# A retention recurrence and a gelu feed-forward on one core: the hand-written order made anew, rows of chunks 3 to 5 over three queues, part 0 of w_in batch by batch in chunk 0

## The chip, the cores and the metric

The kernel runs on one core of one Trainium2 chip. A core has five engines that work side by side: TensorE (PE: matrix products out of SBUF into PSUM banks), VectorE (DVE), ScalarE (ACT), GpSimd (POOL) and SyncE (SP), which here only issues transfers. Each engine executes its own instructions in the order in which the program lists them. Transfers are moved by 16 DMA engines; an engine that issues one puts it in its own queue. The metric is the device time of one execution in microseconds (us), lower is better; the time before is a median of three runs.

## The reference

Two stages follow each other. The first is a recurrence per batch and head with a decay, the second a feed-forward with a tanh gelu on the first one's output. B = 4 batches, H = 8 heads, S = 768 tokens, D = 64.

```python
gamma = 1.0 - 2.0 ** (-5.0 - np.arange(H))
scale = 1.0 / np.sqrt(D)
for t in range(S):
    state = gamma[None, :, None, None] * state + np.einsum('bhd,bhe->bhde', k[:, :, t], v[:, :, t])
    y[:, :, t] = scale * np.einsum('bhd,bhde->bhe', q[:, :, t], state)
x = y.transpose(0, 2, 1, 3).reshape(B * S, H * D)          # 3072 x 512
h = x @ w_in                                               # w_in 512 x 2048
g = 0.5 * h * (1.0 + np.tanh(c * (h + 0.044715 * h * h * h)))   # c = sqrt(2 / pi)
out = g @ w_out                                            # w_out 2048 x 512, out 3072 x 512, f32
```

All inputs are f32. Inside the kernel the products are made in f16 with f32 sums.

## The kernel before

**Tiling.** The 768 tokens are cut into six chunks of 128. In a chunk the recurrence becomes products of 128 tokens with 128 tokens under a triangular mask with the decay in it, and a state of 64 x 64 per head carries what came before. So there are 24 pairs of a chunk c and a batch b. x of a chunk holds all four batches: 512 columns. The feed-forward goes chunk by chunk; w_in and w_out are each cut into four parts j of 512 of the 2048 inner columns.

**The order.** Nothing is scheduled by a compiler. A string, ORDER (lines 16 to 136), lists 1,125 words; the loop at lines 656 to 661 calls a small function for each word, in that order. A word such as `L:k,3,0,A@9` names the function (L), its arguments (row k of chunk 3, batch 0), where there is a choice the engine that does it (A ScalarE, V VectorE, P GpSimd, S SyncE), and behind the `@` the buffers that it takes. So the string sets the order on each engine, the engine of each movable step, the queue of each transfer and which buffer is used again when.

**The steps of the recurrence**, for chunk c and batch b:

- L (306 to 308): a transfer of one 256 KB row of q, k or v, f32, by the queue named. The destination is one of 13 buffers r.
- PREP (318): the row scaled and made f16, or only made f16. q and k give qk.
- T and ET (chunks 0 and 1): qk transposed by TensorE into a bank and copied out. DT (chunks 2 to 5, 343): the same by a DMA transpose, always issued by SyncE.
- A (350): the scores into two banks; EA (358): the banks times mask, on VectorE, one for each of two groups of heads.
- YP (366): what the state gives; YI (382): what the chunk's own tokens give. EY (chunk 0, 400) and EP (chunks 1 to 5, 403) take the result into x.
- SS (411) and ES (424): the new state. For chunks 1 to 5 one ES is four instructions on VectorE.

**The steps of the feed-forward.** LWI and LWO (258, 266) load one part of w_in or w_out, with a change to f16, through GpSimd's queue; HOLD (272) is a tiny transfer by SyncE that reads one part. A product of chunk and part is made in Strassen's manner with seven products of half the size, M1:c,j,1 to 7 (515), in place of eight. They need sums of weights, WI and WO (300, 304), and sums of x, SX:c,1 to 4 (503). Of one chunk and part the seven M1 collect in three banks, X, Y and Z. CP (543) copies a bank to h, D1 (547, VectorE) adds another to it, G (551, ScalarE) makes the gelu: three CP, three D1 and four G for a chunk and part. In chunk 0 a part can also be made without sums, batch by batch: HB:j,b (462) is 16 products into one bank, and GB:j,b,phi (476) two gelus straight from that bank, each half the size of a G. The second product follows for chunk 0 by O0 (570), EO and ST0 (copy and store), for the others by sums SG:c,j,1 to 4 (555) of the gelus, M2 (590, seven products, each in four pieces), CO (a copy, 636), D2 (an addition on VectorE) and ST (the store).

One instruction is counted by TensorE for each column block: an M1 or M2 is four matmuls of 256 columns, an HB 16 of 128, an O0 four of 512. `mm` is line 219, `tt` (additions and scalings) 216, `copy_on` 211 and 213, the gelu 442, the transposes of T 338, so most rows of the profile have one of these lines.

**Around the change.** In the order before, part 0 of w_in in chunk 0 (at M1:0,0,n) is made for all four batches together in seven products, part 1 (HB:1,b) batch by batch, parts 2 and 3 in seven products. The 36 rows of chunks 3 to 5 are all issued by SyncE, and the transposes DT and all HOLD stand in the same queue. The rows of chunks 0 to 2 go over several queues: GpSimd's has, in this order, v,0,3, then part 0, v,0,0, parts 2, 3 and 1 of w_in, six rows of chunk 1, w_out part 0, the row q,1,0 and so on. Two kinds of queue have landing semaphores of their own: eight are shared by the transfers of SyncE and ScalarE in turn, eight serve GpSimd's; a transfer that takes one waits until the transfer that had it before has landed.

Of the kernel before, what the change touches and what calls it, by code (L numbers as in the profile page):

```python
# [40 lines left out]
WI:1,3,V M1:1,3,2@7 O0:0,2 PREP:k,2,3,P@0 D1:1,3,11 O0:0,3 M1:1,1,5@7 G:1,3,11@16 ES:1,0,V EO:0,V@0 M1:1,3,5@2
PREP:k,2,1,A@2 M1:1,3,6 M1:1,0,2@4 CP:1,3,22,A@2 D1:1,1,11 WO:0,1,P G:1,1,11@17 PREP:q,2,3,P SX:1,4,P@1 O0:1,3
DT:2,3@1 CP:1,1,22,V@0 WO:3,1,P D1:1,0,11 PREP:k,2,2,A@3 L:v,2,1,S@6 M1:1,0,6 O0:2,0@6 CP:1,3,12,V@3
PREP:q,2,2,P PREP:v,2,2,P@0 M1:1,0,5@4 PREP:k,2,0,A@4 G:1,0,11@18 M1:1,3,7 M1:1,3,3 PREP:q,2,1,A CP:1,0,12,A@1
WI:1,2,V O0:2,1 PREP:q,2,0,P DT:2,1@2 DT:2,2@3 D1:1,3,22 LD:S D1:1,3,12 M1:1,1,6 EO:1,A@1 DT:2,0@0 HOLD:1,3
M1:1,1,3 L:v,3,3,S@1 WO:3,2,P G:1,3,22@19 CP:1,1,12,A@2 M1:1,0,7 WI:1,4,P G:1,3,12@20 M1:1,3,4 D1:1,1,12
G:1,3,21@21 A:2,3@2,5 M1:1,1,7 M1:1,2,5@7 O0:2,2 M1:1,2,1@1 EA:2,3,1@0 CP:1,0,22,A@3 PREP:v,2,1,P@3 D1:1,0,22
D1:1,1,22 WO:1,2,P G:1,1,12@22 G:1,1,22@23 EA:2,3,0 M1:1,0,3 L:k,3,0,S@2 M1:1,0,4 D1:1,0,12 O0:2,3
CP:1,2,22,V@2 CP:1,2,11,A@0 L:k,3,2,S@8 L:v,3,0,S@3 G:1,0,21@24 M1:1,1,4 M1:1,2,6 L:q,3,3,S@11 A:2,1@5,2
G:1,1,21@25 PREP:v,3,2,P@2 A:2,2@4,3 L:q,4,1,S@7 EO:2,V@2 EA:2,1,0@3 EA:2,2,1@1 G:1,0,22@26 A:2,0@0,6  # L50
CP:1,2,12,A@3 G:1,0,12@27 PREP:v,2,0,P@1 WO:0,2,P EA:2,0,0@2 L:q,3,2,S@5 PREP:v,2,3,P@4 M1:1,2,3 O0:3,0@5
O0:3,1 EA:2,0,1 L:q,3,0,S@4 M1:1,2,7 PREP:k,3,0,A@1 EA:2,1,1 YP:2,0@3,0 EA:2,2,0 L:k,3,3,S@0 L:k,5,1,S@6
# [12 lines left out]
D2:1,11, DT:3,3@6 M1:2,3,3 M1:2,3,4 DT:3,1@0 D1:2,3,12 M1:2,1,1@6 G:2,0,21@14 L:v,4,0,S@10 M1:2,1,2@0
CP:2,1,22,V@3 CO:1,22,A@5 G:2,3,21@4 SG:1,2,4,P@5 CP:2,1,11,A@1 M2:1,6,1,0 M2:1,3,0,0 SG:1,2,3,V@7 M2:1,6,1,1
# [625 lines left out]
```

## Time and profile before

| | before |
|---|---|
| median of the runs, us | 202.04 (201.94 to 203.08, 3 runs) |
| profiled execution, us | 200.09 |
| its span, us | 198.3 |
| mean granted clock of TensorE | 0.98 |
| busy, us (share): TensorE products | 183.0 (92%) |
| VectorE | 160.0 (81%) |
| GpSimd | 139.1 (70%) |
| ScalarE | 119.3 (60%) |

The profile is one execution; its times start at the span's beginning. In the page each engine's busy tenths stand for 40 equal slices of the span, some 5 us each. A row of the timeline gives the start, the time, the engine (PEld is TensorE's loading of weights, an engine name with a q its issuing of transfers), the line, the operation, out<-in with partitions x elements and type, the number of instructions put together, and in brackets the idle time ahead of it with what ended it. In the grouped rows behind the count stand busy us, mean ns of one, and the idle time with its releasers. A row of the chain of waits has the start, the time and what the chain went through. In the stretches, each engine's us and number of instructions are in the order PE, PEld, DVE, ACT, POOL.

### The profile page before, as it was taken

The page shows a single profiled execution, that of the slowest core. Times are in us where ns is not written, and L with a number is a line of the kernel's source. Part 1 is how long each engine was busy: PE and PEld are TensorE (multiplying, and loading weights), DVE is VectorE, ACT ScalarE, POOL GpSimd, SP SyncE. Part 2 cuts the span into 40 slices and gives each one's busy share as a digit, 9 for nine tenths or more (in the row PEclk, how much of TensorE's full clock was granted, in tenths as well). Part 3 has the DMA queues.
Part 4 walks back from the last instruction along what each step waited for, and adds up shares of the span by engine and source line. Part 5 has one row for each costly group of instructions (what it writes and reads, how often), then busy time and mean ns, then how long its engine had stood idle before and what let it go on. Part 6 is the DMA issues. An engine that isn't in the chain of part 4 may idle for free.

```text
span 198.3 us, 5294 instructions
## 1 busy us (share of the span) xinstructions
PE 183.0 (92%) x2111; PEld 149.0 (75%) x2111; DVE 160.0 (81%) x294; ACT 119.3 (60%) x219; POOL 139.1 (70%) x143
## 2 busy tenths in 40 slices
PE   7377999998999999999999699999999999999992
PEld 2155878575676788877978588878888888888882
DVE  0888979899678999998989999998897577674630
ACT  1329798687767477945784669676544745435111
POOL 0797477977999976973799595898359867447200
PEclk9958999999999999999999999999999999999998
DMA  6999999999989999999999995260200201301453
GB/s 144 288 239 243 203 334 234 295 239 333 270 195 235 214 211 258 213 212 216 244 226 190 209 178 155 53 150 27 94 0 0 86 23 58 106 0 56 141 201 136
DMA packets 80540, 34.26 MB, mean 173 GB/s; under 512 B 69060, under 2 KB 78404, under 8 KB 80516
## 3 DMA queue, kind: packets, MB, share of 16 engines
q1 hardware_dynamic: 66164, 19.35, 44.4%
q0 software_dynamic: 6128, 10.23, 21.7%
q10 hardware_dynamic: 8224, 4.36, 7.6%
q8 instruction: 16, 0.26, 0.5%
q14 instruction: 8, 0.07, 0.1%
HBM read 27.63 MB, written 6.29 MB: 171 GB/s over the span
## 4 chain that ended last, share of the span: by engine, by line
PE 65%; DMA 19%; POOL 6%; DVE 4%; issue 2%; ACT 1%; ACTq 0%; SPq 0%; POOLq 0%; DVEq 0%
PE bank L219 65%; DMA w_in<-in_moe_w_in_dram 9%; DMA r<-in_q_dram 6%; DMA qkT<-qk 2%; DVE g L216 2%; DMA r<-in_v_dram 2%; POOL sx L216 2%; POOL t_out L216 1%; POOL qk L216 1%; POOL v L216 1%; DVE h L216 1%; DVE w_out L216 1%; POOL g L216 1%; POOL w_in L262 0%; POOL qk L213 0%
## 5 line engine op out<-in xcount | busy, mean ns | idle before, releaser
L219 PEld LDWEIGHTS <-g 128*128 128x128 f16 x624 | 60.4, 98 | 11.8 <-PE bank L338 0.3
L216 POOL TENSOR_TENSOR g<-g 128x512 f16<-128x512 f16 x46 | 54.5, 1204 | 17.9 <-DVE g L216 7.2
L219 PE MATMUL bank<-w_out,g 128*128 128x256 f16 (+1 forms) x384 | 60.4, 290 | 0.2 <-DMA w_out<-in_moe_w_out_dram 0.2
L216 DVE TENSOR_TENSOR h<-bank,h 128x512 f32<-128x512 f32 x69 | 46.0, 682 | 8.8 <-PE bank L219 4.4
L442 ACT ACTIVATE g<-h 128x512 f16<-128x512 f32 x69 | 42.7, 634 | 15.4 <-DVE h L216 15.0
L219 PEld LDWEIGHTS <-w_in 128*128 128x128 f16 x432 | 39.2, 98 | 6.2 <-issue 0.8
L211 ACT COPY h<-bank 128x512 f32<-128x512 f32 x57 | 32.7, 588 | 13.0 <-PE bank L219 12.6
L219 PEld LDWEIGHTS <-t_in 128*128 128x128 f16 x276 | 26.4, 98 | 9.9 <-issue 4.3
L219 PE MATMUL bank<-t_out,g 128*128 128x256 f16 x240 | 33.4, 273 | 0.0
L216 DVE TENSOR_TENSOR a<-bank,mask 128x512 f16<-128x512 f32 x48 | 30.0, 680 | 3.5 <-PE bank L219 3.4
L219 PE MATMUL bank<-x,w_in 128*128 128x256 f16 (+1 forms) x248 | 29.7, 259 | 0.4 <-DMA w_in<-in_moe_w_in_dram 0.2
L219 PE MATMUL bank<-sx,t_in 128*128 128x256 f16 x184 | 26.5, 273 | 2.3 <-ACT g L442 1.2
L219 PE MATMUL bank<-sx,w_in 128*128 128x256 f16 x184 | 26.7, 273 | 0.0
L216 DVE TENSOR_TENSOR g<-g 128x512 f16<-128x512 f16 x34 | 22.1, 669 | 3.1 <-ACT g L442 2.1
L442 ACT ACTIVATE g<-bank 128x512 f16<-128x512 f32 (+1 forms) x31 | 16.5, 549 | 8.4 <-PE bank L219 5.8
L211 ACT COPY o<-bank 128x512 f32<-128x512 f32 (+1 forms) x19 | 9.7, 516 | 18.2 <-PE bank L219 18.2
L216 POOL TENSOR_TENSOR v<-r,cst 128x512 f16<-128x512 f32 x16 | 16.9, 1061 | 4.0 <-DMA r<-in_v_dram 4.0
L216 DVE TENSOR_TENSOR o<-bank,o 128x512 f32<-128x512 f32 (+1 forms) x18 | 10.6, 595 | 8.9 <-PE bank L219 8.7
L211 ACT CAST qk<-r 128x512 f16<-128x512 f32 x20 | 12.1, 620 | 6.2 <-PE bank L219 2.2
L219 PE MATMUL bank<-x,t_in 128*128 128x256 f16 x92 | 13.8, 273 | 1.9 <-DVE h L216 1.9
L216 DVE TENSOR_TENSOR qk<-r,cst 128x512 f16<-128x512 f32 x13 | 9.2, 744 | 6.5 <-DMA cst<-rr_cst 4.1
L211 ACT COPY qkT<-bank 128x1024 f16<-128x1024 f16 x7 | 6.9, 1013 | 8.0 <-PE bank L338 8.0
(53 smaller groups left out, 191.9 us busy)
## 6 DMA issues: line engine op xcount, KB each, us to landing
r<-in_v_dram SPq DMA_DIRECT2D x15, 256.0 KB, 4.8
r<-in_q_dram SPq DMA_DIRECT2D x15, 256.0 KB, 4.2
r<-in_k_dram SPq DMA_DIRECT2D x14, 256.0 KB, 4.6
out_dram<-o ACTq DMA_DIRECT2D x11, 256.0 KB, 3.8
r<-in_v_dram POOLq DMA_DIRECT2D x9, 256.0 KB, 8.3
out_dram<-o SPq DMA_DIRECT2D x9, 256.0 KB, 2.3
w_in<-in_moe_w_in_dram POOLq DMA_DIRECT2D x8, 256.0 KB, 9.6
r<-in_k_dram POOLq DMA_DIRECT2D x8, 256.0 KB, 8.6
```

What stands on the lines that cost most here:

```text
L211: nc.scalar.copy(out=out, in_=in_)
L216: EN[e].tensor_tensor(out=out, in0=in0, in1=in1, op=op)
L219: nc.tensor.matmul(out=out, lhsT=lhsT, rhs=rhs, start=start, stop=stop, skip_group_check=True)
L442: nc.scalar.activation(out=out, in_=in_, func=AF.Gelu_apprx_tanh, scale=1.0)
```

## The change

Only the string ORDER differs: 121 lines became 120, and every function is as it was (the lines below the string move up by one). The words are in another order almost throughout, and the buffers behind the `@` are others. What was taken out, put in and given to another engine:

- **Part 0 of w_in in chunk 0**: seven M1:0,0,n, three CP:0,0,n, three D1:0,0,n and four G:0,0,n are gone; HB:0,0 to HB:0,3 and the eight GB:0,b,phi come. Parts 0 and 1 are now both made batch by batch. Sums SX of chunk 0 now serve parts 2 and 3 alone.
- **Rows of chunks 3 to 5**: of 36 on SyncE 21 stay; 11 go to ScalarE's queue (k,3,2 q,3,1 k,3,0 k,3,1 q,3,3 v,3,3 v,3,0 v,3,1 k,4,3 q,5,1 k,5,2), 4 to GpSimd's (k,5,1 k,4,2 v,4,2 q,5,3).
- **Late rows of chunk 0**: k,0,3, q,0,3 and v,0,3 go through GpSimd's queue, among the parts of w_in. There the order is now k,0,3 q,0,3, part 0, v,0,3, parts 2, 3 and 1, then five rows of chunk 1 (k,1,0 k,1,1 q,1,1 q,1,2 q,1,0), w_out part 0, k,1,3 k,1,2 q,1,3, w_out parts 1 and 2, the v rows of chunk 1, with a row of chunk 2 and w_out part 3 behind v,1,3. The row q,1,3 was on SyncE before, and w_out's part 2 stood behind the v rows.
- **Other engines for the same steps**, in number of instructions: SX on VectorE 12 to 17, on GpSimd 12 to 7 (SX:1,2 among them); CP on ScalarE 57 to 49, on VectorE 12 to 17; CO on VectorE 7 to 9; ET on ScalarE 7 to 5, on VectorE 1 to 3; WO on VectorE 5 to 7, on GpSimd 11 to 9; PREP on GpSimd 34 to 37, on VectorE 13 to 11, on ScalarE 25 to 24; one SG from GpSimd to VectorE; one EP, EO and EY and one ES of chunk 0 change engines.
- **The end**: the last steps are made by another order of M2 of chunks 4 and 5; the last copy is CO:5,21,A,0 on ScalarE, with ST:5,21,A,0 behind it, where before D2:5,12,1 on VectorE and ST:5,12,S,1 were last.

In all D1 goes from 69 to 66, G from 92 to 88, M1 from 161 to 154, HB from 4 to 8 and GB from 8 to 16; M2 (140) and O0 (16) stay.

The diff at the start and around chunk 1's loads:

```diff
 ORDER = """
-L:k,0,2,A@0 L:q,0,2,A@1 ZERO L:k,0,0,S@2 SPIN:11@0 LI:A L:q,0,3,A@3 LC:S TABLE PREP:k,0,0,V@0 L:k,0,3,A@4
-L:q,0,1,A@5 L:v,0,1,S@6 PREP:q,0,2,P@1 LWI:0 PREP:k,0,2,V L:v,0,3,P@7 MASK L:k,0,1,S@8 L:q,0,0,S@9
...
-EY:0,0,A EY:0,1,A L:k,1,0,P@3 SS:0,0 WI:0,3,V M1:0,0,5@2 M1:0,0,1@7 WI:0,4,V SX:0,2,V@1 SX:0,3,V@2
-CP:0,0,11,A@0 L:k,1,3,P@4 SX:0,4,V@3 L:k,1,2,P@9 M1:0,0,2@5 M1:0,2,1@1 LWO:0 M1:0,0,6 WI:2,1,V CP:0,0,22,A@1
-CP:0,2,11,A@2 D1:0,0,11 M1:0,2,2@4 WI:2,3,V M1:0,2,5@0 M1:0,0,3 CP:0,0,12,A@3 L:q,1,0,P@8 LWO:1 WI:2,2,V
-L:v,1,2,P@5 D1:0,2,11 G:0,0,11@0 CP:0,2,22,A@0 D1:0,0,12 M1:0,0,7 M1:0,2,6 G:0,2,11@1 ES:0,1,A L:v,1,3,P@11
-G:0,0,12@2 D1:0,0,22 L:v,1,1,P@10 L:v,1,0,P@6 M1:0,2,3 M1:0,3,2@5 WI:3,1,V CP:0,2,12,A@2 M1:0,0,4 M1:0,3,1@4
...
+L:k,0,0,S@0 LC:S L:k,0,2,S@1 ZERO L:q,0,0,S@2 PREP:k,0,0,P@0 L:q,0,2,A@3 TABLE L:k,0,3,P@4 PREP:q,0,2,V@1
+L:q,0,1,A@5 PREP:q,0,1,V@2 PREP:k,0,2,V LI:A PREP:q,0,0,V L:q,0,3,P@6 SPIN:11@0 LWI:0 T:0,2@1 L:k,0,1,A@7
...
+YI:0,2@7 EY:0,0,A@0 EA:0,3,1 EY:0,1,A EY:0,2,A L:q,1,1,P@3 HB:0,0@5 L:q,1,2,P@5 SS:0,3 YI:0,3@0 HB:0,2@3
+EY:0,3,V HB:0,3@4 M1:0,2,1@2 ES:0,0,V SX:0,3,V@0 GB:0,3,1@0 M1:0,2,2@7 WI:2,1,V WI:2,2,V ES:0,1,A
+CP:0,2,11,A@0 HB:0,1@0 L:q,1,0,P@1 GB:0,0,1@1 LWO:0 GB:0,2,1 SX:0,1,V@1 L:k,1,3,P@2 M1:0,2,5@6 SX:0,2,V@2
...
+GB:0,3,0@3 M1:0,3,2@7 M1:0,2,3 L:q,1,3,P@8 GB:0,2,0 CP:0,3,11,A@3 M1:0,2,7 GB:0,1,1 HB:1,1@4 LWO:1 WI:0,1,V
+LWO:2 M1:0,3,5@3 WI:3,2,V GB:0,0,0 L:v,1,1,P@4 M1:0,3,6 L:v,1,0,P@9 L:v,1,2,P@6 WI:3,3,V HB:1,0@0 G:0,2,11@4
```

And where chunk 2's products begin, with rows of chunks 3 and 4 (before, then after):

```diff
-O0:3,1 EA:2,0,1 L:q,3,0,S@4 M1:1,2,7 PREP:k,3,0,A@1 EA:2,1,1 YP:2,0@3,0 EA:2,2,0 L:k,3,3,S@0 L:k,5,1,S@6
-YP:2,1@6,2 D1:1,2,12 YI:2,0 SG:1,1,1,P@28 L:q,3,1,S@10 PREP:v,3,3,P@6 L:q,4,2,S@12 SG:1,3,1,P@29 YI:2,1 YI:2,2
...
+EA:2,2,0@2 O0:3,0@6 G:1,1,21@25 EA:2,3,0@1 G:1,0,21@26 PREP:v,2,2,P@1 SG:1,3,1,P@27 M1:1,2,5@2 L:k,3,0,A@0
+A:2,0@0,4 CP:1,2,22,A@3 EA:2,2,1 D1:1,2,11 SG:1,1,1,P@28 L:k,4,0,S@5 A:2,1@1,3 CP:1,2,12,V@1 L:k,3,1,A@2
+O0:3,1 EA:2,3,1 L:q,3,3,A@6 EA:2,1,1@3 EA:2,0,1@0 O0:3,2 PREP:v,2,3,P@3 M1:1,2,3 LD:S EA:2,0,0 M1:1,2,7
...
+L:v,3,3,A@10 WO:2,2,P D1:1,2,22 YI:2,1 SS:2,1 EP:2,0,0,V@0 L:q,4,2,S@4 EP:2,0,1,V YI:2,3 SS:2,2@1 SS:2,3
```

In the built order after, ScalarE's row k,3,1 takes the landing semaphore that SyncE's k,4,0 had, q,3,3 that of the decay table dec (LD), and v,3,3 that of SyncE's q,4,2.

More of the change, by code (lines that the diff above doesn't have):

```diff
@@ new lines @@
+ST:2,21,S M2:3,6,0,1 D1:5,0,11 M1:5,0,6 SX:5,3,P@5 M2:3,6,1,0 M1:5,1,2@3 M2:3,6,1,1 SX:5,4,V@4 D1:5,1,11
+CP:4,2,22,A@1 SG:3,0,3,V@40 G:5,0,11@4 M1:4,3,4 M1:4,2,3 M1:5,0,5@3 CO:3,12,A@1 M2:3,5,0,1 CP:5,0,12,A@2
+CP:5,0,22,V@3 M2:3,7,1,0 M2:3,7,0,0 ST0:2,A G:4,3,21@7 SG:4,1,1,P@0 G:5,1,11@1 M1:5,0,7 ST:3,11,A
+CP:4,2,12,V@0 D1:5,0,22 SG:4,1,2,P@36 D1:4,2,12 M1:5,1,6 G:5,0,22@20 SG:4,3,1,V@24 G:4,2,12@9 M1:5,0,3
+SG:4,0,1,P@11 D1:5,0,12 CO:3,22,A@5 M2:4,2,0,0@6 M2:3,7,1,1 M1:4,2,7 M2:4,1,0,0@4 M1:5,0,4 M1:5,1,5@3
@@ L136 @@
+ST:5,21,A,0
 """
```

211 lines of the change are left out of this document (101 added, 110 removed).

## The prediction

> **What bounds the kernel now.** I read the page first, then the busy times by stretch, then the chain of waits, then the timeline of the stretches in which TensorE is not full. The page, and the stretches (for each engine: us busy and instructions; then clock, DMA share, GB/s):
>
> ```profile
> span 198.3 us, 5294 instructions
> PE   7377999998999999999999699999999999999992
> 0.00:20.00 20.00, 13.23 (x141) 7.50 (x142) 13.14 (x28) 8.67 (x12) 12.61 (x21) 0.83 1.08 228
> 44.00:62.00 18.00, 16.80 (x132) 11.96 (x129) 14.35 (x27) 13.26 (x25) 16.18 (x19) 1.00 0.98 259
> 62.00:85.00 23.00, 22.71 (x286) 18.41 (x284) 22.01 (x43) 17.75 (x34) 20.17 (x19) 1.00 1.04 226
> 85.00:111.00 26.00, 23.46 (x311) 19.65 (x309) 24.32 (x42) 15.03 (x28) 20.11 (x21) 1.00 1.05 219
> 111.00:178.00 67.00, 67.00 (x772) 58.57 (x771) 57.09 (x100) 39.84 (x73) 47.09 (x42) 1.00 0.32 78
> 178.00:195.00 17.00, 16.74 (x154) 14.76 (x151) 6.87 (x15) 5.03 (x12) 4.94 (x5) 1.00 0.40 139
> ```
>
> From 111 us on TensorE has no hole, so only its amount of work counts there. Before that, time is lost in two kinds of place: the start, and holes between 44 and 111 us, where VectorE is busy 46.3 of the 49 us after 62. The profiled execution took 200.09 us, of which 198.3 is span and 1.8 lies around it; the median of the runs is 202.04, so 1.95 is added to a sum made in this trace.
>
> What TensorE's steps cost is read from the distance of weight loads:
>
> ```profile
> 8.09 0.61 PE L338 MATMUL bank<-iden,qk 128*128 128x128 f16 x8 [2.02 <-DMA iden<-rr_ident]
> 19.79 0.39 PE L219 MATMUL bank<-sx,t_in 128*128 128x256 f16 x2 [0.65 <-DVE sx L216]
> 27.10 1.80 PEld L219 LDWEIGHTS <-w_in 128*128 128x128 f16 x32 [0.43 <-issue]
> 43.75 2.35 PE L219 MATMUL bank<-x,w_in 128*128 128x256 f16 x20
> 178.31 16.14 PEld L219 LDWEIGHTS <-g 128*128 128x128 f16 x148
> ```
>
> 148 loads in 16.14 us are 0.109 each, so a step M1 or M2 (four matmuls of 256 columns) is 0.436; 32 loads in 1.80 are 0.056, so HB (16 matmuls of 128) is 0.90; O0, four of 512, is about twice an M1, 0.87.
>
> **Part 0 of w_in.** Seven M1 (3.05 us) go, four HB (3.60) come: +0.55 on TensorE, which nothing hides. On ScalarE and VectorE three CP, three D1 and four G go and eight half-sized GB come; at this stage neither ends the wait.
>
> **The start, up to the first product of chunk 1.** Before, chunk 0's products begin at 19.79 and chunk 1's at 43.75. From the chain of waits the landings of a q row of chunk 0, of w_in's part 1 and of row q,1,0; from the timeline the last cast of chunk 1's v rows; and the prices of VectorE and ScalarE:
>
> ```profile
> 1.26 5.01 DMA r<-in_q_dram
> 15.67 11.33 DMA w_in<-in_moe_w_in_dram
> 27.56 7.10 DMA r<-in_q_dram
> 40.52 0.61 ACT L211 CAST v<-r 128x512 f16<-128x512 f32 x1
> 5.22 1.29 DVE L216 TENSOR_TENSOR qk<-r,cst 128x512 f16<-128x512 f32 x2 [4.09 <-DMA cst<-rr_cst]
> L243 DVE TENSOR_SCALAR mask<-cst 128x128 f32<-128x128 f32 x8 | 2.1, 347 | 0.0
> L213 DVE COPY qkT<-bank 128x1024 f16<-128x1024 f16 x1 | 0.7, 679 | 0.0
> 16.13 2.48 DVE L216 TENSOR_TENSOR a<-bank,mask 128x512 f16<-128x512 f32 x4 [0.68 <-PE bank L219]
> 17.32 2.32 ACT L211 CAST x<-bank 128x512 f16<-128x512 f32 x4
> 20.88 2.05 ACT L211 COPY h<-bank 128x512 f32<-128x512 f32 x4 [1.23 <-PE bank L219]
> ```
>
> In the new order VectorE does five scalings of q and k, ET of batch 0, the mask, ET of batch 1, then EA and q's last scaling. The first q row landed at 1.26 + 5.01 = 6.27; if the second scaling, whose row q,0,1 now stands second in ScalarE's queue as that one did, starts at 7 to 8 us, four of 0.65 (half of 1.29), two ET of 0.68, the mask's 2.1, q's last 0.65 and the five EA that stand ahead of the last YI (0.62 each, a quarter of 2.48) end at 17 to 18; YI, EY (0.58) follow, and HB of batch 0 starts near 18.6. It needs no SX, which cost M1 0.65. That is 1.2 earlier, against 0.55 more work: 0.6 ahead.
>
> It does not last. Part 1 of w_in landed at 15.67 + 11.33 = 27.00 and row q,1,0 at 34.66; between them POOL's queue carried six rows, w_out part 0 and that row. A part has four rows' bytes, so 7.66 us are 11 rows: 0.70 a row, 2.8 a part (worked out from these two). After w_in's part 1, POOL's queue had 11 rows and 2 parts up to the last v row (19 rows, 13.2 us: 40.2, which fits the casts at 40.5). It will have 12 rows and 3 parts, as q,1,3 comes into it from SP and w_out's part 2 stands ahead of v: 16.8 us. One row fewer lies ahead of part 1 (27.0 - 0.7 = 26.3), so v is complete at 43.1. With the cast (0.61) and two EP (0.51 apart, taken from the four copies in 2.05) chunk 1 starts at 44.7, 1.0 later; but one O0 more is done by then (0.87). Net +0.1. If v came 1.5 sooner it would be -1.4; if POOL's queue starts late, +2. I take 0 for part 0 and the start together.
>
> **Holes between 44 and 111.** Their rows (what ended the idle time stands behind):
>
> ```profile
> 47.78 0.88 POOL L308 DMA_DIRECT2D r<-in_v_dram  x1
> 48.68 1.17 POOL L216 TENSOR_TENSOR sx<-sx,x 128x512 f16<-128x512 f16 x1
> 49.90 0.60 PE L219 MATMUL bank<-sx,t_in 128*128 128x256 f16 x4 [1.20 <-ACT g L442]
> 85.83 0.23 PEld L219 LDWEIGHTS <-qkT 64*128 64x128 f16 x8 [0.30 <-DMA qkT<-qk]
> 90.50 0.40 PE L219 MATMUL bank<-qkT 64*128 64x128 f16 x8 [0.34 <-DMA qkT<-qk]
> 92.27 1.04 POOL L216 TENSOR_TENSOR v<-r,cst 128x512 f16<-128x512 f32 x1 [4.04 <-DMA r<-in_v_dram]
> 103.66 0.60 PE L219 MATMUL bank<-sx,t_in 128*128 128x256 f16 x4 [0.42 <-POOL sx L216]
> 104.36 4.50 DVE L216 TENSOR_TENSOR g<-g 128x512 f16<-128x512 f16 x5
> 110.71 0.60 PE L219 MATMUL bank<-x,t_in 128*128 128x256 f16 x4 [1.65 <-DVE h L216]
> ```
>
> At 49.90 TensorE waits for SX:1,2, which ended at 49.85 on POOL behind issues of loads. It moves to VectorE, behind two state updates: -1.0 (0 if VectorE is late, -1.2 at most). The four small waits, for DMA transposes and for SX:3,2, which runs after a POOL that stood 4.04 us for a v row, come from one queue: all 36 rows of chunks 3 to 5 go through SP with the transposes. Of them 21 stay, 11 go to ScalarE, 4 to POOL. Can more queues carry more? To set beside the stretch 62 to 85 above, the stretch in which three queues ran, then SP's issues, their time to landing and ScalarE's price of an issue:
>
> ```profile
> 5.00:10.00 5.00, 1.87 (x17) 0.88 (x17) 4.31 (x11) 1.75 (x3) 3.66 (x5) 0.94 1.28 288
> 57.93 1.23 SPq L345 DMA_TRANSPOSE qkT<-qk  x1
> 64.31 3.92 SPq L308 DMA_DIRECT2D r<-in_q_dram  x4
> r<-in_v_dram SPq DMA_DIRECT2D x15, 256.0 KB, 4.8
> L308 ACTq DMA_DIRECT2D r<-in_k_dram x2: 488/632/776, 0.7 to 4.4; - x2
> ```
>
> From 62 to 85, almost alone, SP's queue moved 226 GB/s; with the other two, from 5 to 10, it was 288. So I count on transposes and rows that come 1 to 4 us sooner: 0.30 + 0.34 + 0.42 go, and of the 1.65 at 110.71, which ends VectorE's backlog after POOL's lateness, 1.3: -2.4 in all, 0 if no time is won. The Trainium skill, DMA: Bandwidth & Descriptors, Issuing engines are not separate DMA queues, says the opposite: all queues end on the same 16 DMA engines, and several issuers save only issue time. By that the 2.4 stays; the 288 against 226 speaks for some gain, the share above 1 for less than it looks.
>
> **What it costs.** An issue on ScalarE takes 0.63 (the row above); 11 are 7 us, eight of them while chunks 1 and 2 overlap. Eight CP fewer (0.51 each) pay 4. ScalarE idles 5.2 of 23 us there, so issues alone hide; but it works in order, and eight landing semaphores serve both hardware queues: in the built order k,3,1 waits until SP's k,4,0 has landed, q,3,3 until dec has, v,3,3 for q,4,2. Behind them stand G and CP, which free banks for M1. I take +0.4 (0 to 4). VectorE gets five SX and five CP more and three D1 fewer:
>
> ```profile
> L216 DVE TENSOR_TENSOR sx<-x 128x512 f16<-128x512 f16 x8 | 3.6, 467 | 0.0
> L213 DVE COPY h<-bank 128x512 f32<-128x512 f32 x12 | 8.2, 682 | 0.9 <-PE bank L219 0.7 <-ACT g L442 0.2
> 194.78 0.43 DVE L216 TENSOR_TENSOR o<-bank,o 128x256 f32<-128x256 f32 x1 [2.20 <-PE bank L219]
> ```
>
> 5 x 0.47 + 5 x 0.68 - 3 x 0.68 = +3.7, and CO and SG come to it too, near the end above all, where it was idle 10 of 17 us. In the tight 62 to 111 about 1 us of it falls: +0.5 there, +0.3 at the end. The last step is now CO on ScalarE instead of the D2 at 194.78, with a store after it as before: 0. Below nothing, this could give 0.5 where POOL's relief counts more; above, 4. The Trainium skill, SBUF — State Buffer, Who interferes with whom, says that a VectorE operation with two SBUF inputs and a GpSimd one that reads SBUF block each other; the five g<-g took 4.50, 0.90 each, which agrees. By it the five SX would cost some 0.43 more each, 2.2 in all.
>
> **Sum.** 0 - 1.0 - 2.4 + 0.4 + 0.8 = -2.2: a profiled 197.9, and 199.8 as a median.
>
> **Rivals.** One: the queues gain nothing. The 16 DMA engines are busy all the time from 62 to 85 (share 1.04), so whichever queue asks, the rows share them and the transposes land no sooner; the 2.4 stays, and -1.0 + 0.4 + 0.8 = +0.2, 202.2, within 1%. Against it speak the 288 GB/s at a share of 1.28. Chance 0.20. The Trainium skill's page named above states this rule. Two, slower: ScalarE stands in its queue at k,3,1 and q,3,3 for SP's rows to land. They take 4.8 from issue; what it keeps free is about 1 us, so one such hold costs 3.8, and rows asked for late cost the 2.4 again. The sum is -1.0 + 3.8 + 0.8 = +3.6, 205.6. It decides once ScalarE reaches k,3,1 within about 3 us of SP's issuing k,4,0; for it speaks the order of waits, against it that k,4,0 stands behind the last transpose of chunk 2, which issued at 57.93, and that this can come earlier. Chance 0.23. Three, slower: v of chunk 1 comes later still, as POOL's queue also waits for its own landings before it issues: +2, with nothing won from the queues +2.2, 204.3. Chance 0.12. That the change does not do what it says: 21 of 36 rows stay on SP, which is in rival one.
>
> **Numbers.** About 1% is what a measurement can tell from no change. The forecast holds 0.45, of which 0.05 lies within 1%, as its -2.2 is just past the bound of 2.0. Faster 0.40; same 0.05 + 0.20 = 0.25; slower 0.23 + 0.12 = 0.35. The range takes the forecast with a start 1.4 better and ScalarE free (199.8 - 2.6, some 197.2), and rival two at the top: 197 to 206. The likeliest case alone is 197 to 201.5.
>
> **What would show it.** Right: TensorE's first w_in product near 18.6, and M1 of chunk 1 near 44.7, with v the last to come; no hole before M1:1,3,6; transposes land within 3 us and no PE row names them; ACT rows show no idle time before a CP that a DMA of r ended. Wrong: ScalarE idle between 60 and 68 us with DMA r as releaser; VectorE's backlog ending PE waits over 2 us; a hole at the end for SG of chunk 5.

## The result, and the profile after

| | before | after |
|---|---|---|
| median of 4 runs each, same chip, us | 201.99 (200.9 to 203.08) | 213.51 (211.05 to 215.74) |
| ratio, 95% interval | | 1.053 (1.0417 to 1.0642) |
| profiled execution, us | 200.09 | 213.65 |
| its span, us | 198.3 | 211.9 |
| mean granted clock | 0.98 | 0.94 |

The change makes the kernel 5.3% slower; forecast were 199.8 us and a range up to 206. Here and below medians take in all runs, while ratios leave out runs of over 1.5% above the fastest of their kernel; where the profiled run was such a one, its own time is given.

The page of the kernel after, its span and its slices of 5.3 us each:

```profile
span 211.9 us, 5348 instructions
PE   7568999998999869608998899999999999999992
DVE  0894897999789799997999999899997767578660
PEclk9855899999999999955999999999999999999998
```

From slice 24 on (122 us) TensorE is as full as before. New are the 6 in slice 15, the 6 and the 0 in slices 17 and 18 (85 to 95 us) and the clock at 5 in slices 18 and 19. The stretches, in the columns of the prediction:

```profile
44.00:62.00 18.00, 17.34 (x163) 12.27 (x157) 15.90 (x32) 14.91 (x29) 15.69 (x16) 1.00 1.03 258
62.00:85.00 23.00, 20.24 (x253) 15.28 (x252) 21.18 (x41) 14.13 (x27) 14.21 (x14) 1.00 0.95 207
85.00:111.00 26.00, 18.17 (x239) 14.70 (x236) 24.00 (x30) 11.12 (x21) 14.35 (x16) 0.80 0.59 146
111.00:125.00 14.00, 12.77 (x120) 10.66 (x117) 13.71 (x21) 8.13 (x16) 13.96 (x14) 1.00 0.93 194
```

From 85 to 111 TensorE is busy 18.17 us and VectorE 24.00. VectorE seems to be the bound, yet it ends only 30 instructions in that time, 42 before: they are longer, not more. How long, and why, the timeline shows (VectorE, GpSimd and TensorE together):

```profile
84.05 0.93 POOL L307 DMA_DIRECT2D r<-in_k_dram  x1
84.51 4.83 DVE L215 TENSOR_TENSOR w_out<-w_out 128x512 f16<-128x512 f16 x1
84.99 1.17 POOL L215 TENSOR_TENSOR g<-g 128x512 f16<-128x512 f16 x1
...
87.40 0.60 PE L218 MATMUL bank<-t_out,g 128*128 128x256 f16 x4
88.20 0.61 POOL L212 CAST qk<-r 128x512 f16<-128x512 f32 x1
88.75 0.93 POOL L307 DMA_DIRECT2D r<-in_k_dram  x1
89.27 4.98 DVE L215 TENSOR_TENSOR g<-g 128x512 f16<-128x512 f16 x1
89.71 1.05 POOL L215 TENSOR_TENSOR v<-r,cst 128x512 f16<-128x512 f32 x1
...
94.90 0.26 PE L218 MATMUL bank<-qkT 64*128 64x128 f16 x1 [6.90 <-DVE a L215]
98.29 1.06 PE L218 MATMUL bank<-w_out,g 128*128 128x256 f16 x4
99.14 1.06 PE L218 MATMUL bank<-sx,t_in 128*128 128x256 f16 x4
101.10 0.61 PE L218 MATMUL bank<-sx,w_in 128*128 128x256 f16 x4
```

The sum WO:3,3 takes 4.83 us and SG:1,0,3 takes 4.98, where such a sum alone takes 0.41. Each is asked for while GpSimd issues one of the four rows that the change gave to it (k,5,1 at 84.05, k,4,2 at 88.75), and lasts through the four GpSimd instructions behind that row (for the first sum from 84.99 to the cast's end at 88.81, two of them left out here). Between 84.51 and 94.17 VectorE does two instructions; A:3,2's banks are not emptied, A:3,3 needs one of them, and TensorE stands 6.90 us. Then its steps are 0.85 apart (98.29 to 99.14) instead of 0.44: the clock fell to half while it stood.

```profile
90.00:91.00 1.00, 0.00 (x0) 0.00 (x0) 1.00 (x1) 0.00 (x0) 1.00 (x2) 0.92 0.37 61
91.00:92.00 1.00, 0.00 (x0) 0.00 (x0) 1.00 (x1) 0.00 (x0) 1.00 (x2) 0.50 0.55 201
100.00:101.00 1.00, 1.00 (x17) 0.77 (x16) 0.22 (x1) 0.58 (x1) 0.00 (x0) 0.50 1.14 259
101.00:102.00 1.00, 1.00 (x13) 0.81 (x10) 0.66 (x2) 0.00 (x0) 0.00 (x0) 0.96 0.86 195
```

Where the 13.6 us of span went follows from a count in both traces: at a time t, t less the price at full clock of all TensorE steps begun by then (0.436 an M1 or M2, 0.87 an O0, 0.89 an HB, less for the small ones) is what TensorE has lost. Whole steps are counted, so a single row is good to about half a us.

| lost, us | before | after | difference |
|---|---|---|---|
| up to 70 us | 18.85 | 18.35 | -0.5 |
| 70 to 88 | 0.81 | 4.60 | +3.8 |
| 88 to 111 | 3.60 | 10.58 | +7.0 |
| 111 to 125 | 0.27 | 1.91 | +1.6 |
| 125 to the last product | 1.21 | 1.74 | +0.5 |
| work itself | 170.01 | 170.51 | +0.5 |
| behind the last product | 3.6 | 4.2 | +0.6 |

### The profile page after: what moved, and what is told of

It reads as the page before. It is cut to its first block, busy times and chain, and to the rows that moved or that the text cites. A ratio compares the mean times of both kernels' runs of the same rounds, so it can differ in the third digit from the quotient of the medians.

```text
span 211.9 us, 5348 instructions
## 1 busy us (share of the span) xinstructions
PE 188.6 (89%) x2147; PEld 153.0 (72%) x2147; DVE 173.9 (82%) x306; ACT 111.8 (53%) x210; POOL 138.4 (65%) x145
## 4 chain that ended last, share of the span: by engine, by line
PE 61%; DVE 19%; POOL 8%; issue 4%; ACT 2%; ACTq 2%; DMA 2%; SPq 0%; DVEq 0%; POOLq 0%
PE bank L218 60%; DVE g L215 5%; DVE h L215 3%; DVE sx L215 3%; DVE a L215 3%; POOL g L215 2%; DMA cst<-rr_cst 2%; POOL w_in L261 2%; POOL qk L215 1%; POOL r L307 1%; DVE t_out L215 1%; ACT g L441 1%; DVE st L429 1%; DVE o L215 1%; ACTq L647 1%
## 5 line engine op out<-in xcount | busy, mean ns | idle before, releaser
L215 POOL TENSOR_TENSOR g<-g 128x512 f16<-128x512 f16 x45 | 52.3, 1178 | 21.7 <-ACT g L441 17.5
L215 DVE TENSOR_TENSOR h<-bank,h 128x512 f32<-128x512 f32 x66 | 43.2, 682 | 12.4 <-PE bank L218 8.2
L218 PEld LDWEIGHTS <-w_in 128*128 128x128 f16 x480 | 42.5, 100 | 8.9 <-DVE sx L215 3.1
L210 ACT COPY h<-bank 128x512 f32<-128x512 f32 x49 | 28.5, 585 | 14.7 <-PE bank L218 14.3
L218 PE MATMUL bank<-x,w_in 128*128 128x256 f16 (+1 forms) x304 | 34.0, 258 | 0.0
L215 DVE TENSOR_TENSOR g<-g 128x512 f16<-128x512 f16 x35 | 25.5, 745 | 2.1 <-ACT g L441 1.9
L441 ACT ACTIVATE g<-bank 128x512 f16<-128x512 f32 (+1 forms) x38 | 18.6, 519 | 16.3 <-PE bank L218 14.9
L218 PE MATMUL bank<-qkT 64*128 64x128 f16 x192 | 10.2, 243 | 9.2 <-DVE a L215 6.9
L212 POOL CAST qk<-r 128x512 f16<-128x512 f32 x11 | 6.6, 614 | 15.1 <-PE bank L218 11.4
L218 PEld LDWEIGHTS <-qkT 64*128 64x128 f16 x192 | 6.5, 104 | 12.9 <-issue 10.5
```

What stands on the lines that cost most here:

```text
L210: nc.scalar.copy(out=out, in_=in_)
L212: EN[e].tensor_copy(out=out, in_=in_)
L215: EN[e].tensor_tensor(out=out, in0=in0, in1=in1, op=op)
L218: nc.tensor.matmul(out=out, lhsT=lhsT, rhs=rhs, start=start, stop=stop, skip_group_check=True)
L441: nc.scalar.activation(out=out, in_=in_, func=AF.Gelu_apprx_tanh, scale=1.0)
```

## The experiments

Two causes stood against each other. Theory one: a row that GpSimd issues among ready work keeps VectorE's additions of two SBUF tiles waiting. Theory two: ScalarE stands at its row issues, waiting for landings (the prediction's second rival). Every experiment but two changes words of ORDER alone; only those are shown. A ratio is to the kernel before, run beside the other.

**GpSimd's four rows to SyncE** (in the kernel after):

```diff
-L:k,5,1,P@10  L:k,4,2,P@2  L:v,4,2,P@1  L:q,5,3,P@11
+L:k,5,1,S@10  L:k,4,2,S@2  L:v,4,2,S@1  L:q,5,3,S@11
```

> The changed kernel with the four rows k,5,1, k,4,2, v,4,2 and q,5,3 issued by SyncE in place of GpSimd, all else as it was. Theory one (a row issued by GpSimd ahead of work that is ready keeps VectorE's operations on two SBUF tiles out for several GpSimd instructions): WO:3,3 and SG:1,0,3 take at most 1.4 us each in place of 4.83 and 4.98, the hole of TensorE at 87 to 95 us goes with the half clock behind it, and the time falls from 213.5 to 203 to 206 us. Rival (GpSimd's dense block of sums does it without the rows, or the time is lost by ScalarE's queue): the two operations stay above 3 us, or the time stays at 211 to 214 us.

Measured: 207.05 (206.19 to 208.01), ratio 1.034 (1.0293 to 1.0387). The timeline of VectorE, the same two sums:

```profile
86.68 0.99 DVE L215 TENSOR_TENSOR w_out<-w_out 128x512 f16<-128x512 f16 x1
87.60 1.26 DVE L215 TENSOR_TENSOR g<-g 128x512 f16<-128x512 f16 x1
```

From 4.83 and 4.98 to 0.99 and 1.26: without the row each waits for about one GpSimd instruction, and the hole of TensorE is gone. The time came out 1 us above what was expected, and 3.4% is still to be explained.

**ScalarE's eleven rows to SyncE** (in the kernel after, GpSimd's left where they are):

```diff
-L:k,3,2,A@9  L:q,3,1,A@3  L:k,3,0,A@0  L:k,3,1,A@2  L:q,3,3,A@6  L:v,3,3,A@10
-L:v,3,0,A@8  L:v,3,1,A@12  L:k,4,3,A@6  L:q,5,1,A@2  L:k,5,2,A@6
+L:k,3,2,S@9  L:q,3,1,S@3  L:k,3,0,S@0  L:k,3,1,S@2  L:q,3,3,S@6  L:v,3,3,S@10
+L:v,3,0,S@8  L:v,3,1,S@12  L:k,4,3,S@6  L:q,5,1,S@2  L:k,5,2,S@6
```

> The changed kernel with the eleven rows of chunks 3 to 5 on ScalarE's queue issued by SyncE. Theory two (ScalarE stands at its row issues until a row of SyncE has landed, 2.7 and 1.5 us at q,3,3 and v,3,3): the loss of 3.3 us of TensorE between 70 and 80 us falls to 1 or less, the stalls of VectorE at 84 to 94 us stay if theory one holds, and the time is 209 to 211.5 us. Rival (the late rows cost what the waits cost): 213 us or more.

Measured: 215.16 (214.1 to 215.5), ratio 1.0726 (1.0687 to 1.0766): slower, a miss. What TensorE lost from 70 to 80 us fell from 3.9 to about 1.5, the way that theory two has it, and the two sums of theory one stayed at 4.83 and 4.98, but a new wait came on VectorE:

```profile
48.32 4.41 DVE L215 TENSOR_TENSOR t_out<-w_out 128x512 f16<-128x512 f16 x1
```

This is WO:3,1, and ahead of it GpSimd issues k,2,1, a row of chunk 2 that was on GpSimd before too. So which sum is caught depends on small shifts, and rows other than the change's four can do it.

**Both at once:**

> The changed kernel with all 36 rows of chunks 3 to 5 issued by SyncE, as the kernel before has them. If the two theories hold and add up: 200 to 203 us, as fast as the kernel before. If the loss is in the new order of VectorE and GpSimd itself: 206 us or more.

Measured: four runs, 202.45, 207.44, 208.06 and 208.52, too far apart for a ratio; three of the four lie where a loss in the new order itself was expected. The profiled one (208.52) has WO:3,1 again, 4.22 us at 48.41. There is no trace of the 202.45, so that this sum was not caught in it is a guess.

**Two rows to GpSimd in the kernel before**, the cause put into the other kernel:

```diff
-L:k,4,3,S@11  L:k,4,1,S@9
+L:k,4,3,P@11  L:k,4,1,P@9
```

> The kernel before with two rows, k,4,3 and k,4,1, issued by GpSimd in place of SyncE; they stand in its dense stretch of sums at 77 to 88 us. Theory one: at least one operation of VectorE on two SBUF tiles in that stretch takes over 2 us, where none took over 1.4, and the time is 203.5 to 209 us. Rival (rows on GpSimd do no harm): all of them stay at or below 1.4 us and the time is 201 to 203 us.

Measured: 202.61 (201.75 to 202.62 but for one run of 210.46), ratio 1.0103 (1.0069 to 1.0136); the time came out under what theory one expected, in the range of its rival, while the sums came out as theory one has them. Timeline of GpSimd, VectorE and TensorE:

```profile
81.29 0.92 POOL L308 DMA_DIRECT2D r<-in_k_dram  x1
83.95 2.19 DVE L216 TENSOR_TENSOR g<-g 128x512 f16<-128x512 f16 x1
85.32 0.91 POOL L308 DMA_DIRECT2D r<-in_k_dram  x1
86.65 2.15 DVE L216 TENSOR_TENSOR t_out<-w_out,t_out 128x512 f16<-128x512 f16 x1
89.03 0.61 PE L219 MATMUL bank<-qkT 64*128 64x128 f16 x8 [3.19 <-DMA qkT<-qk]
```

The two sums, SG:1,2,3 and WO:3,4, took 0.98 and 0.77 in the kernel before and 2.19 and 2.15 here: the row stretches VectorE's sums in the other kernel too, if less. But the hole of 3.2 us behind 85.44 is not theirs. TensorE waits for a transpose of chunk 3, issued up to 83.85, which landed at 88.98, 0.2 us after GpSimd's row k,4,3 (7.5 us after its issue). So a loss of 1% follows from two moved words, and most of it came another way than theory one says: a row on GpSimd's queue and a transpose that land late together. One trace doesn't show which held up the other.

**A fifth row**, k,2,1, to SyncE beside the four:

```diff
-L:k,2,1,P@6
+L:k,2,1,S@6
```

> The changed kernel with five rows, k,5,1, k,4,2, v,4,2, q,5,3 and also chunk 2's k,2,1, issued by SyncE in place of GpSimd; after that no row on GpSimd stands directly ahead of ready work while VectorE has sums to make. Theory one: no operation of VectorE on two SBUF tiles takes over 1.6 us, the runs lie closer together, and the time is 202 to 205.5 us. What is left above the kernel before is then dense contention of single GpSimd operations and the start. Rival (the scatter of the runs and the rest of the loss have another cause): 206 us or more, or runs over 4 us apart.

Measured: 204.7 (203.17 to 209.36), ratio 1.0215 (1.0159 to 1.0272). From 1.053 over 1.034 to 1.0215 the five rows are worth 3.15%, 6.3 us. The profiled run was the 209.36; there the row q,2,0 of chunk 2 did the same to a sum of w_in, three sums in a row taking 5.29 us at 46.32, where none over 1.6 was expected. That k,2,1 costs its 2.5 us by holding up a sum is not shown: the one trace with the four rows on SyncE and k,2,1 on GpSimd (206.19) has no sum of VectorE over 1.4 us.

**Part 0 batch by batch in the kernel before:**

```diff
-M1:0,0,5@2 M1:0,0,1@7 CP:0,0,11,A@0 M1:0,0,2@5 M1:0,0,6 CP:0,0,22,A@1 D1:0,0,11 M1:0,0,3 CP:0,0,12,A@3
-G:0,0,11@0 D1:0,0,12 M1:0,0,7 G:0,0,12@2 D1:0,0,22 M1:0,0,4 G:0,0,21@4 G:0,0,22@5
+HB:0,2@2 HB:0,3@7 GB:0,2,0@4 GB:0,2,1@5 HB:0,0@5 HB:0,1@2 GB:0,3,0 GB:0,3,1
+GB:0,0,0@0 GB:0,0,1@2 GB:0,1,0 GB:0,1,1
```

> The kernel before with part 0 of w_in in chunk 0 made by four HB and eight GB in place of seven M1, three CP, three D1 and four G, all else in its place. As the prediction has it (work +0.55, start earlier as no SX is waited for): within 1 us of the kernel before. Rival (TensorE has no full clock yet at that time, so the HB cost more than 0.9 us each, and the product comes no earlier): 1 to 2.5 us slower.

HB here reads part 0 as WI:0,3 has left it, with a sum in the place of a piece, so the output is not the reference's; the work is of the same amount. Measured: 200.84 (199.78 to 202.16 but for one run), ratio 1.0043 (1.0012 to 1.0074), +0.9 us. The one run, 210.0, is the profiled one, and shows why (GpSimd and VectorE; then stretches):

```profile
47.73 0.89 POOL L308 DMA_DIRECT2D r<-in_v_dram  x1
47.79 9.93 DVE L216 TENSOR_TENSOR w_in<-w_in 128x512 f16<-128x512 f16 x1
```

```profile
50.00:53.00 3.00, 0.16 (x1) 0.00 (x0) 3.00 (x1) 0.00 (x0) 3.00 (x4) 0.93 1.04 323
58.00:63.00 5.00, 4.62 (x19) 2.71 (x19) 3.99 (x10) 3.40 (x7) 0.00 (x0) 0.52 0.00 0
```

One sum, asked for as GpSimd issued v,2,3, waited 9.93 us, through ten GpSimd instructions, and TensorE stood 8.21 us and came back at half clock. So the rows of chunk 2 in the kernel before carry the same hazard; in its own trace no such sum takes over 1.4 us.

**SX:1,2 alone to VectorE, in the kernel before** (`SX:1,2,P@0` to `SX:1,2,V@0`):

> The kernel before with SX:1,2 on VectorE in place of GpSimd, all else in its place. As the prediction has it: the wait of 1.37 us ahead of M1:1,3,6 goes and the time falls by 1.0 us (0.5 to 1.2). Rival (VectorE comes to it late, or the time is lost again at a later wait): 0.3 us or less, or slower.

Measured: 200.49 (198.6 to 201.72), ratio 1.0012 (0.9973 to 1.0052). By 50 us TensorE has lost 1.3 us less than before, at 70 us 0.9 more. WI:1,2 takes 2.69 us at 50.64, but the wait that takes the gain back, ahead of A:2,0, is for a transpose of chunk 2:

```profile
63.39 0.40 PE L219 MATMUL bank<-qkT 64*128 64x128 f16 x8 [2.10 <-DMA qkT<-qk]
```

SyncE began to issue it at 57.99, in the kernel before at 57.93; it landed at 63.34 instead of 61.67. Why it landed later is open.

**Pairs, measured by themselves.** Behind the kernel before, code was added in which GpSimd makes a sum, issues a row or not (by GpSimd, by SyncE, two rows), and makes 5 or 8 ready sums, while VectorE, released by the first sum, makes copies from a bank and then one sum of two SBUF tiles.

```diff
+        tt("P", x, y, data[10], ALU.add)
+        if row:
+            for e in row:
...
+                L("k", 0, 0, e)
+        for n in range(runs):
+            tt("P", scr[n], data[10], data[11], ALU.add)
+        for _ in range(halves):
+            half(x)
+        tt("V", x, data[10], data[11], ALU.subtract)
```

> The kernel before, and behind its own work 22 cases one after the other, each with a run of GpSimd's sums that are all ready (1.15 us each) and one operation of VectorE on two SBUF tiles (0.41 alone) asked for at a known place in it; the output is the reference's, the time some 200 us longer. Cases: no row ahead of the run; a row issued by GpSimd ahead of it, VectorE's operation asked for before, in the middle, at the end or behind the row's issue; two rows; the row issued by SyncE; runs of 2, 5 and 8 sums. Theory one: without a row on GpSimd, and with the row on SyncE, VectorE's operation waits for the running sum alone (at most 1.4 us in all); with a row asked for ahead of the run it waits for several sums (over 2 us; with a run of two about 2.5). If it is starved for as long as GpSimd has ready work, a run of eight gives some 9 us; if only for what GpSimd has queued, four sums or 5 us as with a run of five. Rival (GpSimd's dense runs do it without a row): all cases are alike.

Timeline of GpSimd and VectorE, a row with five sums behind it, a row issued by SyncE, and a row with eight:

```profile
195.83 0.92 POOL L308 DMA_DIRECT2D r<-in_k_dram  x1
196.38 6.24 DVE L216 TENSOR_TENSOR t_in<-t_in,t_in 128x512 f16<-128x512 f16 x1
196.76 5.56 POOL L216 TENSOR_TENSOR t_in<-t_in,t_in 128x512 f16<-128x512 f16 x5
204.40 0.90 DVE L216 TENSOR_TENSOR t_in<-t_in,t_in 128x512 f16<-128x512 f16 x1
241.97 9.54 DVE L216 TENSOR_TENSOR t_in<-t_in,t_in 128x512 f16<-128x512 f16 x1
242.35 8.88 POOL L216 TENSOR_TENSOR t_in<-t_in,t_in 128x512 f16<-128x512 f16 x8
```

Asked for at 196.38, the VectorE sum ended at 202.62, when the five GpSimd sums had ended (202.32); with eight sums, at 251.51 (251.23). With SyncE issuing the row it took 0.90, with none 0.42 and 0.44, all in a first pass through the eleven cases. The count over both passes is less clean than the theory as first put. With a row of GpSimd directly ahead, eleven of 16 sums took 3.74 to 9.54 us; the five others, 0.43 to 1.08, are the cases with two rows, those with a run of two (about 2.5 was expected) and one of the two that were asked for as the issue began (the other took 6.67). Without such a row the three cases of the second pass took 4.22, 4.87 and, with SyncE issuing the row, 5.33 us. GpSimd had not paused there since an earlier row of its own, which the next experiment leaves out.

**The same pairs, no row on GpSimd anywhere:**

> As pairs_after_before, but no row is issued by GpSimd in any case: 16 cases with runs of 8, 5 and 2 ready sums, VectorE's operation asked for at once, in the first, second, third or fourth sum; in one case a row is issued by SyncE. If the row on GpSimd is the cause: VectorE's operation waits for the running sum alone in every case, at most 1.6 us in all. If long runs of ready sums do it by themselves: some cases over 2 us.

```profile
196.55 64.59 POOL L216 TENSOR_TENSOR t_in<-t_in,t_in 128x512 f16<-128x512 f16 x57 [0.76 <-DVE t_in L216]
198.19 0.90 DVE L216 TENSOR_TENSOR t_in<-t_in,t_in 128x512 f16<-128x512 f16 x1
231.37 1.47 DVE L216 TENSOR_TENSOR t_in<-t_in,t_in 128x512 f16<-128x512 f16 x1
```

GpSimd makes 57 sums without a pause in the stretch shown and goes on so to the last case, and in all 16 cases VectorE's sum took between 0.41 and 1.47 us (0.90 in the two with a row from SyncE). So a dense run of GpSimd is not enough: without a row of GpSimd earlier in the run the long waits do not occur. With one they mostly do; what else they need is open.

**Three rows of chunk 2 to SyncE, in the kernel before** (`L:v,2,0`, `L:q,2,0`, `L:v,2,3`, P to S):

> The kernel before with three rows of chunk 2, v,2,0, q,2,0 and v,2,3, on SyncE in place of GpSimd. SX:1,2 on GpSimd no longer stands behind their issues (2.6 us), and no row stands ahead of GpSimd's ready work there. Expected: the wait of 1.37 us ahead of M1:1,3,6 goes, runs over 2 us above the median no longer occur, and the time falls by 0.5 to 1.3 us. Rival (it is lost again at a later wait, as with SX:1,2 on VectorE): no difference over 0.3 us.

Measured: 202.06 (200.97 to 202.57 but for one run of 313.53), ratio 1.0042 (1.0009 to 1.0075). A miss: if anything slower by 0.4%. The trace kept is of the 313.53, in which the mean clock was 0.563, so it does not show where the waits avoided were lost again.

**The same with SX:1,2 on VectorE:**

> The kernel before with SX:1,2 on VectorE and the three rows v,2,0, q,2,0 and v,2,3 on SyncE. With SX:1,2 alone 1.3 us were won by 50 us and lost again at 61 us behind an operation of VectorE that waited 2.69 us after a row of GpSimd. If that starvation is what lost it: 0.7 to 1.5 us faster than the kernel before, with no operation over 1.6 us. If the rows on SyncE delay the transposes of chunk 2, as their 0.4% alone may mean: no faster, or slower by up to 1 us.

Measured: 201.76 (201.14 to 203.0), ratio 1.005 (1.0019 to 1.0081). No gain, though no such sum takes over 1.4 us now. TensorE stands elsewhere instead: 0.81 us at 43.73 for a part of w_out, 0.79 and 1.09 for sums of x on GpSimd (M1:1,3,3 and M1:3,0,6) and 1.18 ahead of A:3,2 for a transpose.

**Ten rows off GpSimd, in the kernel after**, its four and six of chunk 2, with three sums moved ahead or behind a neighbour in VectorE's order:

```diff
-L:k,5,1,P L:k,4,2,P L:v,4,2,P L:q,5,3,P L:k,2,1,P L:k,2,3,P L:v,2,3,P L:v,2,2,P L:k,2,0,P L:q,2,0,P
+L:k,5,1,S L:k,4,2,S L:v,4,2,S L:q,5,3,S L:k,2,1,S L:k,2,3,S L:v,2,3,S L:v,2,2,S L:k,2,0,S L:q,2,0,S
```

(SX:2,4 and SX:2,3 now stand right behind SX:2,2, and SG:1,3,4 ahead of SG:2,3,3.)

> The changed kernel with ten rows on SyncE in place of GpSimd (the four of chunks 3 to 5 and k,2,3, v,2,3, v,2,2, k,2,0, q,2,0, k,2,1 of chunk 2, so that no row stands ahead of ready work on GpSimd any more), and on VectorE SX:2,4 and SX:2,3 directly behind SX:2,2, SG:1,3,4 ahead of SG:2,3,3. If what is left of the loss after five rows is starvation now and then and sums that stand behind others: no operation of VectorE on two SBUF tiles over 1.6 us, the waits ahead of M1:2,0,3 (2.04) and M2:1,3,1,0 (2.26) go, 200.5 to 203 us with runs within 2.5 us. If it is the start and the amount of VectorE's work: 203.5 us or more.

Measured: 205.55 (203.79 to 207.86), ratio 1.0193 (1.0137 to 1.025). No sum of VectorE takes over 2.11 us now. The time is 2.5 us above the range expected; the 0.2% below the five rows lies within the intervals.

**That, and ScalarE's eleven rows to SyncE too:**

> As ten_rows_and_sums, and the eleven rows on ScalarE go to SyncE too. This is the three queues of the change measured without starvation. As the prediction has it, three queues gain 2.4 us and cost 0.4: this kernel would be 2 us slower than ten_rows_and_sums. Rival one (all queues share the same DMA engines): within 0.7 us of it. Theory two (ScalarE stands at its row issues): 0.7 to 2.5 us faster.

Measured: 203.81 (202.29 to 205.09), ratio 1.0134 (1.0072 to 1.0196). One hole over 2 us is left before 111 us, for a sum of w_out that stands late in VectorE's order:

```profile
93.06 0.81 PE L218 MATMUL bank<-w_out,g 128*128 128x256 f16 x6 [2.10 <-DVE w_out L215]
```

**That sum, WO:1,3, moved up behind WO:2,3**, in the two kernels just above (a: ten rows; b: ten rows and ScalarE's):

> As ten_rows_and_sums, and WO:1,3 on VectorE directly behind WO:2,3 in place of behind SG:2,3,3. If the wait of 2.26 us ahead of the second half of M2:1,7,0,0 is for this sum and is not made up later: 2 us faster than ten_rows_and_sums (ratio to before 1.01 in place of 1.019). If it is made up later, no difference over 0.7 us.

> As ten_rows_scalar_to_sync, and WO:1,3 on VectorE directly behind WO:2,3. The same as in weights_sum_early_a: 2 us faster than ten_rows_scalar_to_sync (ratio to before 1.003 in place of 1.0134). Against weights_sum_early_a: if ScalarE's row issues cost time, 0.7 to 2 us faster; if the first difference of 1.7 us was scatter, within 0.7 us; if three queues gain, slower.

Measured: a 204.88 (203.36 to 205.79), ratio 1.0188 (1.0141 to 1.0235); b 202.28 (201.39 to 204.3), ratio 1.009 (1.0053 to 1.0127). Both miss the 2 us expected: 0.1 and 0.9 us, by ratios whose intervals overlap. In a the hole went, and the wait at 81 us grew from 1.73 to 2.39. a and b differ in ScalarE's rows alone: 2.0 us (0.0098 of 201), intervals apart. In b TensorE's longest wait between 60 and 112 us is this:

```profile
93.50 0.60 PE L218 MATMUL bank<-x,t_in 128*128 128x256 f16 x4 [1.03 <-DVE h L215]
```

**In b, also three sums WO of GpSimd behind PREP:k,2,1:**

> As weights_sum_early_b, and GpSimd's WO:2,1, WO:1,2 and WO:0,2 behind its PREP:k,2,1, which waits for a row, so that they don't run beside SX:1,1 and SX:1,2 on VectorE. If the waits of 1.18 and 0.57 us ahead of M1:1,3,6 and M1:1,0,5 come from these sums beside each other: 0.7 to 1.5 us faster than weights_sum_early_b, as fast as the kernel before or up to 0.5 us faster. Rival: lost later, within 0.5 us of weights_sum_early_b.

Measured: 203.03 (202.7 to 204.45), ratio 1.0114 (1.007 to 1.0158): no gain. No version of the new order was faster than before.

## Why the prediction was wrong

**Part 0 of w_in** (+0.55): about right. Alone it costs 0.9 us, with an interval of 0.2 to 1.5 in which the forecast lies. Not priced was the clock: in the trace after the first products run while it is still at half, and HB of batch 0 takes 1.89 us in place of 0.90 (before, the clock was at 1.00 from 17 us on).

```profile
19.00:22.00 3.00, 3.00 (x40) 2.57 (x37) 0.22 (x1) 0.89 (x2) 2.90 (x4) 0.50 1.24 205
```

**The start** (taken 0, by its sum +0.1): right in the number, not in the path.

```profile
19.07 1.89 PE L218 MATMUL bank<-x,w_in 128*128 128x128 f16 x16
45.45 2.35 PE L218 MATMUL bank<-x,w_in 128*128 128x256 f16 x20
49.33 0.61 PE L218 MATMUL bank<-sx,t_in 128*128 128x256 f16 x4 [0.24 <-DVE sx L215]
```

HB of batch 0 starts at 19.07 (forecast 18.6), chunk 1 at 45.45 (44.7); at 44 us the new order has lost 17.55 against 17.27, +0.3. But v,1,3, the last v row of chunk 1, landed at 41.73, 1.4 us before the 43.1 of the forecast, and the 1.4 that the prediction would have given for that did not come: from 19.5 to 50 us TensorE waits 0.2 us in all, so chunk 1 began when the work ahead of it was done. That the sum still came out near is luck.

**Holes between 44 and 111**, SX:1,2 (-1.0): right where it stands, wrong as a gain. The wait of 1.20 ahead of 49.90 became 0.24 ahead of 49.33, and at 50 us TensorE is 0.9 better than before. But the experiment with this word alone gave 1.0012: it was lost again at 63 us, at a wait for a transpose. A hole's length is what is won at the hole, not at the end.

**Holes**, three queues (-2.4): this is the step that failed, together with "What it costs". The waits it named did go. No row of TensorE between 44 and 111 us has a transfer as releaser, and GpSimd's sixteen scalings of v waited for rows 0.7 us in all, where one alone had waited 4.04:

```profile
L215 POOL TENSOR_TENSOR v<-r,cst 128x512 f16<-128x512 f32 x16 | 17.1, 1076 | 0.8 <-DMA r<-in_v_dram 0.7
```

Yet version b, with all 36 rows of chunks 3 to 5 on SyncE, has no wait of TensorE for a transfer there either, so these waits go without the further queues. What the queues added was a loss, 3.8 us by GpSimd's four rows and 1.2 to 2.0 by ScalarE's eleven. The prediction gave the four rows on GpSimd no price at all: its +0.8 for VectorE, 4 at most, was for more sums and copies, and no term was for a sum that meets GpSimd's work behind a row. The four additions beside those rows, each of 0.41 alone, are 4.83, 4.98 and twice 2.24:

```profile
113.62 2.24 DVE L215 TENSOR_TENSOR sx<-x,sx 128x512 f16<-128x512 f16 x1
116.39 2.24 DVE L215 TENSOR_TENSOR g<-g 128x512 f16<-128x512 f16 x1
```

Over all VectorE additions of two f16 tiles in SBUF, time above 0.41 each is 12.0 us for 66 before, 22.2 for 74 after, 15.3 with the four rows on SyncE, and 13.7 in b. The Trainium skill, SBUF — State Buffer, Who interferes with whom, has a VectorE instruction with two SBUF inputs contend with a GpSimd one that reads SBUF for a port pair that is an exclusive lock, and says of VectorE's two-port modes that whoever issues first holds it for the whole instruction; waiting for one instruction of the other agrees with the pairs without a row (1.47 at most), and disagrees with those behind one (9.54, eight instructions). The estimate of 2.2 in all, made by that rule and left out of the sum, stands against 10.2 us more (22.2 less 12.0).

**What it costs**, ScalarE (+0.4, to 4; rival two +3.8): ScalarE does stand at its row issues, as rival two says, but not for the landings that it names, and at about half its price. ScalarE's issues in the trace after:

```profile
64.88 2.70 ACTq L307 DMA_DIRECT2D r<-in_q_dram  x1
67.63 0.63 ACT L441 ACTIVATE g<-h 128x512 f16<-128x512 f32 x1 [2.73 <-POOL t_out L215]
67.93 1.53 ACTq L307 DMA_DIRECT2D r<-in_v_dram  x1
69.52 1.73 ACTq L587 DMA_DIRECT2D out_dram<-o  x1
```

q,3,3 holds ScalarE 2.70 us where a row takes 0.37 to 0.63; v,3,3 (1.53) and a store (1.73) follow. By the updates of their semaphores in this trace dec had landed at 63.24, before q,3,3's issue began at 64.88, and q,4,2 at 64.23, before v,3,3's at 67.93; the buffers that the two rows take were free by 56.2. So neither waited for what the prediction had named. Both issues ended soon after the oldest row still under way in ScalarE's own queue had landed: at 67.58 and 69.45, with q,3,1 landing at 67.44 and k,3,0 at 69.28. That points to the queue's own backlog, but v,3,0 went out in 0.37 us at 71.66 with three transfers of that queue under way, so the cause stays open. The sign I had named, idle time with a DMA as releaser, did not come either: the wait lies inside the issue, and the gelu's releaser reads as GpSimd. The eleven rows are worth 2.0 us (a against b) or 1.2 (0.0059 between the two kernels without WO:1,3 moved, whose intervals overlap).

**The last step** (0): 0.6 more lies behind the last product than before.

**Rivals.** Two was on the right side, for a smaller loss than the main one and with another wait than it said. One, that the queues gain nothing, is right in its rule as far as the runs show it: the stretch 62 to 85 moved 207 GB/s, 226 before, though a kernel that waits more also asks for less. The Trainium skill's rule in DMA: Bandwidth & Descriptors, Issuing engines are not separate DMA queues, agrees. But 202.2 supposed that asking from another engine is nearly free. Three, v of chunk 1 later still, did not come: v came earlier. None held the main cause.

**The account**, of 5.3%, or 10.6 us, in the order of undoing (each the difference of two ratios, by 201): GpSimd's four rows 3.8; k,2,1 2.5; the other five rows and the three sums 0.4; ScalarE's rows 1.2; WO:1,3 0.9; and b's 1.8 that are left, of which part 0 is 0.9 and some 0.9 stays open. The 0.4, the 1.2 and WO:1,3's 0.9 lie within the overlap of their intervals. The terms need not add: ScalarE's rows, taken out first, made it slower.

## What to carry to other kernels

Before a transfer is given to GpSimd, look at what stands behind it: if several of its instructions are ready, and VectorE has an addition of two SBUF tiles meanwhile, price that addition at the whole run, not at one instruction; moving the row to SyncE took the long waits away wherever no other row of GpSimd stood ahead. A row issued by an engine that also computes can hold that engine, here for up to 2.70 us, and this shows as a long issue, not as idle time. In an order that is this tight, a hole that is closed is a gain only when the run says so: SX:1,2 on VectorE closed one of 1.2 us and won nothing that could be measured.

## What the runs showed of the hardware

A row issued by GpSimd ahead of ready work kept an addition of VectorE waiting up to 9.93 us, through ten of GpSimd's instructions; why a row does that, and why it did not with two rows in succession or with a run of two, is open.

TensorE's clock fell to half about 3 us after its last product had ended (88.00 to 91 in the trace after) and was back at 101, 6 us after TensorE resumed at 94.90. The Trainium skill, TensorE: Matmul & The Clock Gate, Part 1: The HAM clock gate, gives some 3.4 us or more for each way; falling came near that, and coming back took longer with work that had gaps. So the hole of 6.90 us cost about 10 in all (22.95 lost at 88 us, 32.91 at 100).
